# Sliding-window attention with expert routing: the fourth batch's q and k cast and turned earlier, second expert layer let in later

## The chip, the cores and the metric

The kernel runs on one core of a Trainium2 chip. The metric is the device time of one execution in microseconds (us). A core has five engines that run their own instruction queues side by side: TensorE (PE, matrix products), VectorE (DVE), ScalarE (ACT), GpSimd (POOL) and SyncE (SP, which here only issues DMAs). Each takes its instructions in the order of the program and waits on semaphores for what other engines and DMAs produce.

## What is computed

Two stages, of which the second reads the first's result:

```
# attention: q, k, v of shape (8 batches, 8 heads, 576, 64)
scores = q @ k^T / sqrt(64) + slope_h * -(i - j)     where 0 <= i - j < 128, else -1e9
attn   = softmax(scores);  x = attn @ v              -> x: (4608 tokens, 512)
# routing and experts: w1 (8, 512, 1024), w2 (8, 1024, 512)
P = exp(x @ w_gate - max); 8 times: normalise rows, normalise columns, scale by 4608/8
out = sum over e of P[:, e] * (relu(x @ w1[e]) @ w2[e])
```

## The kernel before

**Tiling.** Each batch has 576 rows: four blocks of 128, and a tail of 64. The loop runs over `steps = (b, kb, u)`: 8 batches, 5 key blocks, 2 halves of the heads. One step is a half-block, numbered `at = 2 * kb + u` from 0 to 9 within its batch; "(2, 3)" is half-block 3 of batch 2, and batches are counted from 0, so "batch 3" is the fourth. A half-block has `scores` (PE) and `exps` (ACT, L417) for the step after, `masks` (DVE, L430: the exponentials times a table that holds the window and the slopes) and `values` (PE, L455) with its division (DVE, L465 and L466). When a block is done its rows `xsb` are transposed into `xT` (by PE and a DVE copy, L497, for batches 0 to 2 and 7; by DMA, L499, for the others).

**q and k.** They come as float32 in `load_qk` (two DMAs of 1 MB on SP, L258), are cast to fp16 in four head pairs each by `cast_qk` (q on DVE, L274; k on ACT, L276; two q casts of batches 1 and 2 on POOL, L272), and must be transposed. For batches 0 to 2 PE does it (`turn_pe`, L338). From batch 3 on (`XPE = 3`) two DMA transposes on SP do it (`turn_qk`, L288), and `order_qk` (L299) then puts columns in order: four copies on POOL for k (`kN`) and four on DVE for q (`qN`, two each behind half-blocks 6 and 7). The 64-row tails are loaded by `load_tail` (L247), cast on POOL (L306) and turned by DMA (L307) in `turn_tail`.

**Filler.** PE's spare time in the attention half is filled with the first two experts' products. A unit is four blocks of tokens (two for the first two units): eight layer-1 atoms (L103, four matmuls each, relu on ACT L115 or DVE L111), then layer-2 atoms (L125, copied out by DVE L527 or L533, stored by SP L519 three outputs later from a ring of six buffers, the name `yo`). `Filler.fill(us)` hands out atoms until a planned cost (`L1_US`, `L2_US`: 0.87 and 1.74 us for a full unit) is reached. Each half-block calls it twice, first with 1.0 and then with the rest of a budget, the planned cost of all work that is ready divided by the half-blocks that are left. As long as `filler.hold` is true no layer-2 atom is handed out. For the first two units a layer-2 atom is half a block's: four matmuls, planned at 0.87 us.

**Order.** Nothing reorders the program: each engine's queue is the order of this text. Casts and turns of the next batch stand at the end of a half-block, behind its `values`, its filler work and its v load (L361); v blocks are cast on POOL (L371) one batch ahead.

Of the kernel before, what the change touches and what calls it, by code (L numbers as in the profile page):

```python
# [14 lines left out]
def kernel(  # L15
# [139 lines left out]
    XPE, YO = 3, 6  # L155
# [60 lines left out]
    if True:  # L216
# [23 lines left out]
        def spin_alone(n):  # L240
            spins[0] += 1
            spin(aps.tile([P, GT], FP32, name=f"psJ_{spins[0]}", tag="pmm", bufs=4), n)
# [21 lines left out]
        def cast_qk(b, j, which=(1, 0), pool=False):  # L264

            if b not in c16s:
                c16s[b] = per.tile([P, 2, RI, H, Dh], FP16, name=f"c16_{b}", tag="a8", bufs=8)
            for n in which:
                src = raw[b][n][:, 2 * j : 2 * j + 2, :].rearrange("p h (i d) -> p i h d", i=RI)
                to = c16s[b][:, n, :, 2 * j : 2 * j + 2, :]  # L270
                if pool:
                    nc.gpsimd.tensor_copy(out=to, in_=src)  # L272
                elif n == 0:
                    nc.vector.tensor_copy(out=to, in_=src)  # L274
                else:
                    nc.scalar.copy(out=to, in_=src)  # L276
# [52 lines left out]
        def turn_pe(b, kq, j):  # L329

            wide = j == NDT
            ps = aps.tile([P, RI, P], FP32 if wide else FP16, name=f"psT_{b}_{kq}_{j}", tag="pmm", bufs=4)
            for i in range(RI):
                if wide:
                    src = tails[b][:, 2 * i : 2 * i + 2, :]
                else:
                    src = c16s[b][:, kq, i, 2 * j : 2 * j + 2, :]
                nc.tensor.matmul(  # L338
                    out=ps[:, i, :],
                    lhsT=src.rearrange("p h d -> p (h d)"),  # L340
                    rhs=ident32 if wide else ident,
                    is_transpose=True,
                    start=(i == 0),
                    stop=(i == RI - 1),
                )
            if wide:
                nc.scalar.copy(out=QKT[b][2], in_=ps)
                return
            to = QKT[b][kq][:, j].rearrange("p (r i) -> p r i", i=RI)
            if kq == 0:  # L350
                nc.vector.tensor_copy(out=to, in_=ps.rearrange("p i r -> p r i"))
            else:
                nc.scalar.copy(out=to, in_=ps.rearrange("p i r -> p r i"))
# [36 lines left out]
        def scores(b, kb, u):  # L390

            nk, nn = sizes(kb)
            ps = aps.tile([P, 2, 2, 2 * P], FP32, name=f"psS_{b}_{kb}_{u}", tag="psS", bufs=2)
            both = kb < NKB - 2
            for y in range(2):
                j = 2 * u + y
                for hb in range(2):
                    n = 2 * P if both else nk
                    nc.tensor.matmul(  # L399
                        out=ps[0:nk, hb, y, 0:n],  # L400
                        lhsT=cols(b, 1, j, hb, kb),
                        rhs=cols(b, 0, j, hb, kb, 1 + both),
                    )
                for hb in range(2):
                    if nn and not both:
                        nc.tensor.matmul(
                            out=ps[0:nk, hb, y, nk : nk + nn],
                            lhsT=cols(b, 1, j, hb, kb),
                            rhs=cols(b, 0, j, hb, kb + 1),
                        )  # L410
            pss[b, kb, u] = ps
# [61 lines left out]
        def by_pe(b):  # L473
            return b < XPE or b == B - 1
# [192 lines left out]
        for n, (b, kb, u) in enumerate(steps):  # L667
            nxt = steps[n + 1] if n + 1 < len(steps) else None
            at = 2 * kb + u
            left = ((8 if b < XPE else 10) - at) % 10 + 1  # L670
            budget = filler.backlog() / (11 if (b, at) == (XPE, 0) else left)
            if b == 0:
                budget = 0.0
            if nxt:
                if nxt[0] < XPE and nxt[1:] == (RI - 2, 1):
                    turn_pe(nxt[0], 0, NDT)
                if nxt == (1, 0, 0):
                    filler.ready = RI
                    spin_alone(6)
                    for _ in range(NFT):  # L680
                        filler.take()
                    cast_qk(1, 0)
                    cast_qk(1, 1)
                    for j in range(NDT):
                        turn_pe(1, 1, j)
                        turn_pe(1, 0, j)
                        if j < 2:
                            cast_qk(1, j + 2, (1,))
                        filler.take()
                if nxt == (2, 0, 0):  # L690
                    filler.fill(11.0)
                    cast_qk(2, 0)
                    cast_qk(2, 1)
                    for j in range(NDT):
                        turn_pe(2, 1, j)
                        turn_pe(2, 0, j)
                        if j < 2:
                            cast_qk(2, j + 2, (1,))
                        filler.fill(1.0)
                if n == 0:  # L700
                    scores(*nxt)
                elif nxt[2] == 0:
                    scores(*nxt)
                    scores(*nxt[:2], 1)
                exps(*nxt)
            got = filler.fill(1.0) if b else 0.0
            if nxt:
                masks(*nxt)
            values(b, kb, u)
            if n > 0 and u == 0 and by_pe(steps[n - 1][0]):  # L710
                turn_x(*steps[n - 1][:2])
            if u == 1 and n // 2 + NKB < B * NKB:
                cast_v(n // 2 + NKB)
            filler.fill(budget - got)
            if at == 0 and b > XPE:
                filler.ready = 4 * b
            if at < 8 and b < XPE:
                filler.ready = 4 * b + at // 2
            if at == 8 and b < XPE:
                filler.ready = 4 * b + 4  # L720
            if u == 1 and not by_pe(b):
                turn_x(b, kb)
            if u == 1:
                if kb == 1 and b > 0:
                    gates(4 * b - 4, 4 * b)
                if n // 2 + NKB + 1 < B * NKB:
                    load_v(n // 2 + NKB + 1)
            if b == 0 and at == 5:
                load_weights(1)
            if (b, at) == (1, 8):  # L730
                filler.allowed.add(1)
            if (b, at) == (1, 5):
                for j in (2, 3):
                    cast_qk(2, j, (0,), True)
            if (b, at) == (1, 1):
                filler.hold = False
            if (b, at) == (0, 9):
                load_qk(2, 2)
            if (b, at) == (0, 7):
                homes(1)  # L740
            if (b, at) == (1, 3):
                homes(2)
            if 1 <= b < B - 2 and at == 3:
                load_qk(b + 2)
            if XPE <= b + 1 < B - 1 and at >= 8:
                cast_qk(b + 2, at - 8)
            if XPE <= b + 1 < B:
                late = 2 if b + 1 == XPE else 0
                if late and at < 2:
                    cast_qk(b + 1, at)  # L750
                if late <= at < late + 2:
                    cast_qk(b + 1, at - late + 2)
                if at == late + 1:
                    turn_qk(b + 1)
                    order_qk(b + 1, 1, range(NDT))
                if at == 5:
                    turn_tail(b + 1)
                if at in (6, 7):
                    order_qk(b + 1, 0, range(2 * at - 12, 2 * at - 10))
            if b < B - 1 and at == (1 if b > 1 else 5) and b:  # L760
                load_tail(b + 1)
            if 10 * b + at >= 66:
                i = 10 * b + at - 66
                if i % 8 == 0:
                    home_last(2 + i // 8)
                (load_w2 if i % 8 < 4 else load_w1)(2 + i // 8, i % 4, 4)
            if (b, at) == (7, 0):
                todo += sums_of(2, *extras(2))
            if b == 7 and at >= 5:
                some(1)  # L770
# [270 lines left out]
        for n in range(N):  # L1041
# [5 lines left out]
            if late:  # L1047
                finish(units[n - 2][0])
                late = []
# [16 lines left out]
            if ends(n - 1):  # L1066
                late = pairs[2] + pairs[3]
# [37 lines left out]
```

## Time and profile before

| | us |
|---|---|
| three runs | 1060.18, 1054.64, 1059.56 (median 1059.56) |
| the profiled execution | 1057.3 |
| its span, first to last instruction | 1055.4 |
| PE busy in it | 1037.4 |
| DVE, ACT, POOL busy | 633.4, 433.5, 82.3 |
| mean granted PE clock | 0.998 |

In the profile a row of a timeline is: start in us, duration in us, engine, source line, operation, output<-input, partitions x elements and type, number of instructions merged, and in brackets the engine's idle time before it with what ended that wait. A row of a window table is: the window, its length, the busy time of each engine (with instructions), the granted clock as a share of full speed, DMA share, GB/s. SPq rows are DMA issues on SP's queue: the duration is that of the issue, not of the transfer.

Batch 1 begins at about 33 us, batch 2 at 72, batch 3 at 107; attention ends near 280 us, and the rest is the remaining six experts.

### The profile page before, as it was taken

What the parts mean: (1) busy time and instruction counts of PE and PEld (TensorE: products, weight loads), DVE (VectorE), ACT (ScalarE), POOL (GpSimd) and SP (SyncE); (2) the same over time, 40 slices, a digit from 0 to 9 for tenths busy, and PEclk for the clock granted to TensorE, in tenths of its full rate; (3) what the DMA queues carried; (4) which work ended last, traced back from release to release, by engine and by line L of the source; (5) the groups of instructions that cost most, each with busy time, mean ns of one, the idle gap of its engine ahead of it and who ended that gap; (6) DMA issues with size and microseconds to landing.
All of it is one profiled execution on the core that took longest, in us unless ns stands there. A gap on an engine that the chain in (4) does not pass through costs nothing.

```text
span 1055.4 us, 21220 instructions
## 1 busy us (share of the span) xinstructions
PE 1037.4 (98%) x9042; PEld 802.5 (76%) x9042; DVE 633.4 (60%) x1170; ACT 433.5 (41%) x718; POOL 82.3 (8%) x143
## 2 busy tenths in 40 slices
PE   8899999999999999999999999999999999999998
PEld 5545444444444888888888888888888888888887
DVE  5726566655687665655655655655655555556555
ACT  7555554555332333333333333333333333333332
POOL 1212133334100000000000000000000000000000
PEclk9999999999999999999999999999999999999999
DMA  9995598969991510210210220220220220220240
GB/s 254 222 245 151 98 208 214 205 141 176 193 207 55 111 46 26 71 53 19 71 60 13 71 65 8 71 55 16 71 69 3 71 71 2 71 70 2 71 91 20
DMA packets 166174, 98.55 MB, mean 93 GB/s; under 512 B 85024, under 2 KB 157504, under 8 KB 166080
## 3 DMA queue, kind: packets, MB, share of 16 engines
q1 hardware_dynamic: 151344, 79.21, 29.1%
q0 software_dynamic: 14304, 17.84, 10.6%
q8 instruction: 70, 1.15, 0.4%
q10 hardware_dynamic: 432, 0.16, 0.1%
q14 instruction: 24, 0.20, 0.1%
HBM read 87.74 MB, written 19.02 MB: 101 GB/s over the span
## 4 chain that ended last, share of the span: by engine, by line
PE 84%; DMA 1%; DVE 0%; issue 0%; SPq 0%; DVEq 0%
PE psh L892 35%; PE psS_m L947 31%; PE psy L125 8%; PE psh L103 8%; PE psN L455 1%; DMA pbc<-ptd 1%; PE psS L399 1%; PE psy L1012 0%; PE psG L505 0%; DVE yo L533 0%; DVE aux L876 0%; PE psX L486 0%; PE psC L817 0%; DVE pt L430 0%; PE psP L832 0%
## 5 line engine op out<-in xcount | busy, mean ns | idle before, releaser
L899 ACT ACTIVATE hs<-psh 128x512 f16<-128x512 f32 x432 | 257.9, 597 | 453.6 <-PE psh L892 372.6
L892 PE MATMUL psh<-aux,w1l 128*128 128x256 f16 x2880 | 372.6, 273 | 0.5 <-DVE aux L876 0.5
L892 PEld LDWEIGHTS <-w1l 128*128 128x128 f16 x2880 | 281.5, 98 | 33.9 <-issue 0.8
L947 PEld LDWEIGHTS <-hs 128*128 128x128 f16 x2568 | 251.0, 98 | 29.3
L904 DVE TENSOR_TENSOR hs<-hs 128x1024 f16<-128x1024 f16 x107 | 74.1, 693 | 274.4 <-ACT hs L899 274.4
L947 PE MATMUL psS_m<-w2l,hs 128*128 128x256 f16 x1440 | 186.6, 273 | 0.0
L103 PE MATMUL psh<-xT,w1t 128*128 128x512 f16 (+1 forms) x608 | 141.5, 372 | 2.8 <-DVE xT L497 2.4
L125 PE MATMUL psy<-w2t,hT 128*128 128x512 f16 x576 | 134.3, 380 | 1.4 <-DMA w2t<-in_moe_w_dram 1.4
L876 DVE TENSOR_TENSOR aux<-xT,pbc 128x1024 f16<-128x1024 f16 x108 | 131.6, 1219 | 2.8 <-DMA pbc<-ptd 2.8
L115 ACT ACTIVATE hT<-psh 128x512 f16<-128x512 f32 (+1 forms) x144 | 83.5, 586 | 107.0 <-PE psh L103 106.5
L125 PEld LDWEIGHTS <-hT 128*128 128x128 f16 x576 | 53.5, 98 | 62.3 <-DMA w2t<-in_moe_w_dram 1.5
L103 PEld LDWEIGHTS <-w1t 128*128 128x128 f16 x608 | 55.2, 99 | 54.9 <-issue 8.3
L533 DVE CAST yo<-psy 128x512 f16<-128x512 f32 x68 | 46.8, 690 | 62.9 <-PE psy L125 62.6
L417 ACT ACTIVATE pt<-psS 128x1024 f16<-128x1024 f32 (+2 forms) x80 | 67.7, 852 | 39.0 <-PE psS L399 33.0
L993 DVE TENSOR_TENSOR acc<-acc,psS_m 128x256 f32<-128x256 f32 (+1 forms) x162 | 74.4, 505 | 12.3 <-PE psS_m L947 11.1
L947 PE MATMUL psS_m<-more,hs 128*128 128x256 f16 x576 | 74.7, 273 | 0.0
L892 PE MATMUL psh<-aux,w1t 128*128 128x256 f16 x576 | 74.7, 273 | 0.0
L907 DVE TENSOR_TENSOR hs<-hs 128x1024 f16<-128x1024 f16 x107 | 73.2, 684 | 0.0
L430 DVE TENSOR_TENSOR pt<-pt,mask 128x1024 f16<-128x1024 f16 (+2 forms) x80 | 53.0, 663 | 33.2 <-ACT pt L417 33.1
L892 PEld LDWEIGHTS <-w1t 128*128 128x128 f16 x576 | 56.3, 98 | 6.6
L568 POOL DMA_DIRECT2D w2t<-in_moe_w_dram x2 | 1.8, 878 | 705.6 <-PE psS_m L947 670.1
L455 PEld LDWEIGHTS <-pt 128*128 128x128 f16 (+2 forms) x576 | 28.2, 100 | 26.3 <-DVE pt L430 7.7
(89 smaller groups left out, 675.2 us busy)
## 6 DMA issues: line engine op xcount, KB each, us to landing
pbc<-ptd SPq DMA_DIRECT2D x108, 128.0 KB, 4.3
y<-ysp SPq DMA_DIRECT2D x36, 256.0 KB, 4.6
ysp<-yo SPq DMA_DIRECT2D x68, 128.0 KB, 2.9
v<-in_v_dram SPq DMA_DIRECT2D x32, 256.0 KB, 4.6
out_dram<-acc SPq DMA_DIRECT2D x31, 256.0 KB, 2.5
q<-in_q_dram SPq DMA_DIRECT2D x5, 1024.0 KB, 6.2
k<-in_k_dram SPq DMA_DIRECT2D x5, 1024.0 KB, 9.2
w2t<-in_moe_w_dram POOLq DMA_DIRECT2D x4, 1024.0 KB, 12.5
```

Of the source, the lines that this page charges most:

```text
L103: nc.tensor.matmul(out=ps[:, 0:nt], lhsT=w1ts[e][:, dt, P * ft : P * ft + P], rhs=xT[:, b0 : b0 + nb, dt, :], start=(dt == 0), stop=(dt == ...
L115: nc.scalar.activation(out=st["hT"][:, ft, 0:nt], in_=ps[:, 0:nt], func=AF.Relu)
L125: nc.tensor.matmul(out=ps, lhsT=st["hT"][:, ft, P * ms : P * ms + P], rhs=w2ts[e][:, ft, :], start=(ft == 0), stop=(ft == NFT - 1),)
L417: nc.scalar.activation(out=pt[0:nk, :, 0 : nk + nn], in_=ps[0:nk, :, :, 0 : nk + nn].rearrange("p a y n -> p (a y) n"), func=AF.Exp, scale ...
L430: nc.vector.tensor_tensor(out=pt[0:nk, :, 0:w], in0=pt[0:nk, :, 0:w], in1=mask[0:nk, hs, 0:w], op=ALU.mult)
L876: nc.vector.tensor_tensor(out=xs(n).rearrange("p (d b t) -> p d b t", d=NDT, b=2), in0=xT[:, 2 * g : 2 * g + 2].rearrange("p b d t -> p d ...
L892: nc.tensor.matmul(out=ps[:, f, :], lhsT=W1L[e][:, dt, P * ft : P * ft + P], rhs=xs(n)[:, HB * dt : HB * dt + HB], start=(dt == 0), stop=( ...
L899: nc.scalar.activation(out=h[n][:, 2 * i : 2 * i + 2, :], in_=ps, func=AF.Relu)
L904: nc.vector.tensor_tensor(out=t[:, NFT : NFT + NF2, :], in0=a[:, 0:NF2, :], in1=a[:, NF2:NFT, :], op=ALU.add)
L907: nc.vector.tensor_tensor(out=t[:, NFT + NF2 : 2 * NFT, :].rearrange("p f n -> p (f n)").rearrange("p (f t) -> p f t", t=P), in0=a[:, :, P ...
L947: nc.tensor.matmul(out=Ms[g, bank][:, half, :], lhsT=left(n, m, f), rhs=W2L[e][RIGHT[m]][:, f, :], start=(e == 2 and f == 0 and half == 0) ...
L993: nc.vector.tensor_tensor(out=a, in0=a, in1=p2, op=op)
```

## The change

Two edits in the loop over half-blocks. First, `filler.hold` is cleared at the end of half-block 2 of batch 1 instead of half-block 1. Second, the casts of batch 3 during batch 2: before, one head pair of q and k at the end of each of half-blocks 0, 1, 2 and 3, and the DMA transposes and POOL copies at the end of half-block 3. After, head pairs 0, 1 and 2 at the end of half-block 0, head pair 3 at the end of half-block 1, and there the transposes and the POOL copies. For batches 4 to 7 the calls and their places stay as they were.

```diff
-            if (b, at) == (1, 1):
+            if (b, at) == (1, 2):
                 filler.hold = False
...
             if XPE <= b + 1 < B:
-                late = 2 if b + 1 == XPE else 0
-                if late and at < 2:
-                    cast_qk(b + 1, at)
-                if late <= at < late + 2:
-                    cast_qk(b + 1, at - late + 2)
-                if at == late + 1:
+                if at == 0 and b + 1 == XPE:
+                    cast_qk(b + 1, 0)
+                    cast_qk(b + 1, 1)
+                if at < 2:
+                    cast_qk(b + 1, at + 2)
+                if at == 1:
                     turn_qk(b + 1)
                     order_qk(b + 1, 1, range(NDT))
```

## The prediction

> **What bounds the kernel now.** I read the page first, then the table of ten-microsecond windows, then the timelines of the engines around the place where half-blocks of batch 2 are cast and where batch 3 begins.
>
> ```profile
> span 1055.4 us, 21220 instructions
> PE 1037.4 (98%) x9042; PEld 802.5 (76%) x9042; DVE 633.4 (60%) x1170; ACT 433.5 (41%) x718; POOL 82.3 (8%) x143
> ```
>
> TensorE (PE) is busy for 1037.4 of 1055.4 us. All that a reordering can win is the 18 us in which PE stands, and time in which it runs at a reduced clock. The second half of the kernel does not change at all, so the place to look is the attention half, and there the windows show one that stands out:
>
> ```profile
> 10.00:20.00 10.00, 8.23 (x111) 5.10 (x109) 7.92 (x19) 8.50 (x12) 4.16 (x10) 1.00 1.25 208
> 90.00:100.00 10.00, 10.00 (x94) 5.38 (x92) 4.43 (x11) 5.95 (x10) 0.33 (x1) 1.00 0.68 138
> 100.00:110.00 10.00, 7.41 (x70) 3.83 (x68) 9.42 (x20) 2.29 (x4) 6.73 (x9) 1.00 0.21 57
> 110.00:120.00 10.00, 9.65 (x58) 4.12 (x56) 3.44 (x9) 6.11 (x10) 1.78 (x4) 0.83 0.25 65
> ```
>
> The columns are PE, weight load, DVE, ACT, POOL, then the granted clock and DMA. From 100 to 110 us PE is busy 7.41 of 10 us, the least of the eighteen windows up to 180 us, while DVE is at 9.42; just before, DVE is at 4.43. From 110 to 120 the mean clock is 0.83, which over 10 us is 1.7 us of PE time lost. No other window there shows a clock under 1.00. This is the end of batch 2 and the start of batch 3, in PE's own order:
>
> ```profile
> 104.88 0.31 PE L455 MATMUL psN<-v,pt 128*64 128x65 f16 x4
> 106.25 0.31 PE L455 MATMUL psN<-v,pt 64*64 64x65 f16 x4 [1.07 <-DVE pt L430]
> 107.03 1.07 PE L399 MATMUL psS<-qN,kN 64*128 64x256 f16 x8
> 109.47 1.02 PE L103 MATMUL psh<-xT,w1t 128*128 128x512 f16 x4 [1.38 <-DVE xT L497]
> 110.91 4.45 PE L103 MATMUL psh<-xT,w1t 128*128 128x512 f16 x12
> 115.20 0.29 PE L455 MATMUL psN<-v,pt 128*128 128x65 f16 x4
> 150.39 2.59 PE psh L103 x12
> ```
>
> PE waits 1.07 us for a mask product and 1.38 us for the copy of the last transposed block into xT. Then twelve 512-wide matmuls stretch from 110.91 to 115.20, 4.29 us, where twelve like them take 2.59 elsewhere: 1.70 us too long, the loss which the clock column shows. So 2.45 us of waits and 1.70 us of clock, 4.15 us together, lie at this joint.
>
> Why DVE is late is in its own rows:
>
> ```profile
> 96.69 0.56 DVE L430 TENSOR_TENSOR pt<-pt,mask 128x768 f16<-128x768 f16 x1 [1.32 <-ACT pt L417]
> ...
> 100.47 0.69 DVE L533 CAST yo<-psy 128x512 f16<-128x512 f32 x1 [1.03 <-PE psy L125]
> 101.08 1.07 DVE L430 TENSOR_TENSOR pt<-pt,mask 128x768 f16<-128x768 f16 x1
> ...
> 102.95 2.03 DVE L299 COPY qN<-qk 128x512 f16<-128x512 f16 x2
> ...
> 105.50 0.70 DVE L430 TENSOR_TENSOR pt<-pt,mask 64x256 f16<-64x256 f16 x1
> ...
> 106.67 1.09 DVE L299 COPY qN<-qk 128x512 f16<-128x512 f16 x2
> ...
> 108.27 0.27 DVE L430 TENSOR_TENSOR pt<-pt,mask 64x256 f16<-64x256 f16 x1
> ...
> 109.01 0.41 DVE L497 COPY xT<-psX 128x512 f16<-128x512 f16 x1
> ```
>
> The same mask product of 128x768 takes 0.56 us at 96.69 and 1.07 at 101.08. The pair of qN copies takes 1.09 us at 106.67 and 2.03 at 102.95. The 64x256 mask takes 0.27 us at 108.27 and 0.70 at 105.50. The long ones all lie where POOL works on batch 3's kN copies or on what stood behind them:
>
> ```profile
> 99.67 4.85 POOL L299 COPY kN<-qk 128x512 f16<-128x512 f16 x4 [9.95 <-DMA qk<-c]
> ```
>
> Excess on DVE: 0.51 + 0.94 + 0.43 = 1.88 us, in one unbroken queue from 100.47 to the xT copy at 109.01.
>
> **The change, part 1: when batch 3 is turned.** The text of the change speaks of pairs; the code puts three casts of each of q and k (head pairs 0, 1, 2) behind half-block 0 and the fourth behind half-block 1, with both DMA transposes and the four POOL copies. No instruction is added or removed.
>
> ```profile
> 81.21 0.42 DVE L274 CAST c<-q 128x512 f16<-128x512 f32 x1
> 82.98 0.69 DVE L533 CAST yo<-psy 128x512 f16<-128x512 f32 x1 [1.35 <-PE psy L125]
> ...
> 84.74 0.42 DVE L274 CAST c<-q 128x512 f16<-128x512 f32 x1
> ...
> 92.08 0.42 DVE L274 CAST c<-q 128x512 f16<-128x512 f32 x1
> ```
>
> On DVE the cast at 81.21 is followed by 1.35 us of idle; two more casts of 0.42 fit, 0.84 us, so the next one (82.98) is not late. The last q cast then is the one at 84.74, ending at 85.16, where before it was that at 92.08, ending at 92.50. That is 7.34 us earlier.
>
> ```profile
> 79.43 0.63 ACT L276 CAST c<-k 128x512 f16<-128x512 f32 x1
> 80.93 1.02 ACT L417 ACTIVATE pt<-psS 128x1024 f16<-128x1024 f32 x1 [0.87 <-PE psS L399]
> ...
> 107.46 1.02 ACT L417 ACTIVATE pt<-psS 128x1024 f16<-128x1024 f32 x1 [3.35 <-PE psS L399]
> ```
>
> On ACT two more casts of at most 0.63 stand behind the one at 79.43 and end by 81.3; the exponential that started at 80.93 after 0.87 us of idle moves by up to 0.4 us. The mask that uses it waited on DVE behind the output copy at 82.98 anyway, so I cost this at nothing; without that cover it would be 0.4 us.
>
> ```profile
> 73.13 1.24 SPq L247 DMA_DIRECT2D t<-in_q_dram  x1
> ...
> 75.14 6.51 SPq L519 DMA_DIRECT2D ysp<-yo  x2
> ...
> 82.87 0.84 SPq L258 DMA_DIRECT2D k<-in_k_dram  x1
> 92.52 4.65 SPq L288 DMA_TRANSPOSE qk<-c  x2
> ```
>
> SP is an in-order queue. The transposes waited for the last cast and started at 92.52; now they start at 85.2 and hold SP for 4.65 us, to 89.9. They have moved ahead of the tail loads (73.13), the y stores (75.14), a v load and batch 4's q and k loads (82.87), so all of these now issue after 89.9. The k load needs
>
> ```profile
> k<-in_k_dram SPq DMA_DIRECT2D x1, 1024.0 KB, 9.2
> ```
>
> 9.2 us to land. Issued at about 93 it is there at 102.2; its first reader is an ACT cast ahead of the exponential at 107.46, which moves to about 105.6. That leaves 3 us, so I cost it at nothing. The stores are priced among the rivals.
>
> POOL gets the copies 7.34 us earlier: 92.3 to 97.2 instead of 99.67 to 104.52. The v casts queued behind them feed batch 3, which begins about 107 us, and the one ahead-of-time cast that now waits behind them has as long. DVE, at 4.43 of 10 us in that window, has room for a slowdown of the size seen, 1.88 us, without PE noticing.
>
> Without the excess, DVE's queue from 100.47 reaches the 64x256 mask at about 104.1 and PE, at 104.88, goes straight on: the wait of 1.07 is gone. The xT copy, ending at 109.42, ends at 107.54. PE gets there at about 106.3, since the scores at 107.03 need the second pair of qN copies, which end at 107.76 - 1.88 = 105.9. So a wait of 1.2 us stays, and the matmul of 109.47 starts at 107.6. **Gain 1.9 us**; bounds 0 (what POOL casts then slows DVE as much) and 2.45 (both waits vanish).
>
> [...]
>
> **Part 2: the clock.** PE's matmul at 109.47 starts after a stretch of 4.6 us with 2.45 us of waits. With 1.25 us less idle, the window from 100 to 110 would have PE busy some 8.66 of 10 us; the window from 10 to 20 has 8.23 and a clock of 1.00. I take the drop to vanish: **1.70 us**; bounds 0 and 1.70.
>
> **Part 3: layer 2 one half-block later.** At half-block 2 of batch 1 the filler gives one layer-2 atom (four matmuls):
>
> ```profile
> 37.10 0.29 PE L455 MATMUL psN<-v,pt 128*128 128x65 f16 x4
> 38.78 1.04 PE L125 MATMUL psy<-w2t,hT 128*128 128x512 f16 x4 [1.38 <-DMA w2t<-in_moe_w_dram]
> ```
>
> It waits 1.38 us for w2. Now the filler gives nothing there, since layer 1 has run out. Eight atoms of 0.87 are owed by the planner's own costs, 6.96, and the budget is what is owed over the half-blocks left: in half-block 3 that is 6.96/6 = 1.16 us, one atom; in half-block 4 it is 6.09/5 = 1.22, of which 0.35 is left after the first atom, enough by its rule for a second one. From half-block 5 on the order is the old one. So one atom moves by two half-blocks. PE then waits at the old place for other things:
>
> ```profile
> 37.65 0.68 DVE L430 TENSOR_TENSOR pt<-pt,mask 128x1024 f16<-128x1024 f16 x1
> ...
> 38.45 0.42 DVE L466 TENSOR_TENSOR xsb<-psN,rden 128x256 f16<-128x256 f32 x1
> ```
>
> The mask ends at 38.33, so PE waits from 37.40 to 38.4, 0.95 to 1.0 us instead of 1.38, and again 0.25 us or so for xsb, ready at 38.87. The moved 0.87 us are spent later, in front of no wait that would hide them. **Gain 0.3 us**, near 1.38 - 1.0; bounds -0.9 (the atom uncovered at its new place and nothing won) and 1.38.
>
> Sum: 1.9 + 1.7 + 0.3 = 3.9 us. The profiled execution took 1057.3 us (1055.4 of span and 1.9 around it), so 1053.4. The three runs have a median of 1059.56; the four times known (1060.18, 1054.64, 1059.56, 1057.3) have a mean of 1057.9. Taking the 3.9 off that I forecast **1054.0 us**.
>
> **Rivals.** *The clock drops all the same.* For it: a wait of 1.2 us stays at the same place. Against it: windows with as little PE work kept a clock of 1.00. It would leave 2.2 us, thus 1055.7. [...]
>
> *The contention moves along.* POOL's v casts, kept back by the early copies, fall on the same DVE stretch, or masks in the quiet window become the wait. Against it: DVE's 4.43 of 10. Then only part 3 remains: 1057.6.
>
> *Slower: the stores behind the transposes.* Outputs rotate through six buffers; the output copied on DVE at 100.47 needs the buffer whose store is the first at 75.14. A store lands
>
> ```profile
> ysp<-yo SPq DMA_DIRECT2D x68, 128.0 KB, 2.9
> ```
>
> 2.9 us after issue. Behind transposes (to 89.9) and two tail loads (at most 1.24 each) it lands by about 96, 4.5 us ahead of need. It decides from 4.5 us more on SP. That SP can be held is shown by a single load in batch 1:
>
> ```profile
> 49.15 10.07 SPq L258 DMA_DIRECT2D q<-in_q_dram  x1
> ```
>
> If each transpose took 10.07 us, SP would be 15.5 us later, the copy at 100.47 would wait 11 us, and masks queue behind it: 1057.3 + 11 - 0.3 = 1068. Against it: they took 4.65 for both.
>
> *It does not do what it says:* the casts still end with half-block 3's. The queue order excludes this unless ACT or DVE were full there; they are not.
>
> **How the numbers follow.** Forecast 0.56; clock drops 0.22; contention moves 0.13; stores 0.06; the rest 0.03. One half percent, 5.3 us, is about what a measurement of this kernel can tell from no change; the runs before differ by 5.5 us. Against the median 1059.56 the forecast is 5.6 us faster, against the mean 3.9, so a little under half of the forecast's chance (0.25) is faster by over 0.5%, and of the clock's rival a quarter (0.06): 0.31. Slower by over 0.5%: the stores and a little of the contention case, 0.08. Within: 0.61. The range runs from 1050.5 (the lowest run, 1054.64, less 3.9 and rounded) to 1059.0 (the contention case, 1057.6, and 1.4 for the spread of runs); it takes in the bounds of the parts.
>
> **What would show it.** Transposes on SP starting near 85 and kN copies on POOL near 92; in the window 100 to 110 no 1.07 us mask and no 2.03 us qN pair; PE's first layer-1 matmul of batch 3's start near 107.3; a clock of 1.00 from 110 to 120; no PE wait on w2, and four matmuls more behind half-block 4 of batch 1. Wrong would be: copies early but the xT copy as late as ever; a clock under 1.00 at another place; SP issuing the stores after 96.

## The result and the profile after

| | median, us | runs | lowest to highest |
|---|---|---|---|
| before | 1059.37 | 18 | 1054.64 to 1061.93 |
| after | 1054.63 | 18 | 1052.86 to 1058.07 |

The ratio, of the means (1054.72 to 1059.02), is 0.9959, with a 95% interval of 0.9948 to 0.9971: 4.3 us, 0.41% faster, where 1054.0 and 3.9 us were forecast. The ratio itself lies within the 0.5% that was called the bound; its interval reaches just beyond it. One execution of before among the 35 that stand beside e1 to e4 below was slow throughout (1795.9 us, mean clock 0.556) and is left out of every comparison.

The profiled execution of after took 1058.07 us, the slowest of the 18, so its span is no shorter than that of before. From the page of after:

```profile
span 1055.2 us, 21217 instructions
PE 1037.0 (98%) x9042; PEld 803.7 (76%) x9042; DVE 632.4 (60%) x1170; ACT 433.9 (41%) x718; POOL 81.0 (8%) x143
```

Ten-microsecond windows of after (columns as in the table of before):

```profile
40.00:50.00 10.00, 9.10 (x104) 5.33 (x103) 5.81 (x15) 4.10 (x5) 5.19 (x12) 0.83 0.93 210
90.00:100.00 10.00, 10.00 (x106) 5.63 (x106) 5.26 (x13) 6.28 (x10) 3.94 (x4) 1.00 1.03 199
100.00:110.00 10.00, 9.37 (x82) 4.89 (x79) 8.64 (x21) 3.32 (x6) 3.42 (x8) 1.00 1.02 274
110.00:120.00 10.00, 8.87 (x60) 4.13 (x60) 4.48 (x13) 6.70 (x12) 1.65 (x4) 1.00 0.22 59
```

The window from 110 to 120 has a clock of 1.00 instead of 0.83. The window from 100 to 110 has PE busy for 9.37 us instead of 7.41, but this trace runs late, so that part of the joint has moved out of that window. In a second profile of the same kernel (f1_whole below), which runs less late, it is 8.71, near the 8.66 of the forecast:

```profile
100.00:110.00 10.00, 8.71 (x80) 4.58 (x78) 8.56 (x21) 2.46 (x5) 2.05 (x5) 1.00 1.07 267
```

But in the first profile the clock is 0.83 from 40 to 50, in batch 1, and a clock under 1.00 at another place is one of the signs that the prediction named for being wrong. The timelines of POOL and PE of after show what happened there:

```profile
40.18 0.61 POOL L371 CAST v<-v 128x512 f16<-128x512 f32 x1 [8.32 <-DMA v<-in_v_dram]
40.90 0.55 PE L455 MATMUL psN<-v,pt 128*128 128x65 f16 x7 [2.90 <-POOL v L372]
```

POOL sat idle for 8.32 us until the DMA of a v block landed, and PE waited 2.90 us for the cast. Batch 2 and all behind it therefore stand some 3 us later in this trace than they would otherwise (batch 1 takes 39.73 us here and 36.48 in f1, as read below); this lies well ahead of the joint of batches 2 and 3. At the joint itself, PE's timeline reads:

```profile
107.94 0.56 PE L455 MATMUL psN<-v,pt 128*64 128x65 f16 x8
...
108.75 0.61 PE L399 MATMUL psS<-qN,kN 64*128 64x256 f16 x8
110.70 1.02 PE L103 MATMUL psh<-xT,w1t 128*128 128x512 f16 x4 [1.34 <-DVE xT L497]
...
112.14 2.76 PE L103 MATMUL psh<-xT,w1t 128*128 128x512 f16 x12
114.75 0.29 PE L455 MATMUL psN<-v,pt 128*128 128x65 f16 x4
```

The row of 107.94 stands for those of 104.88 and 106.25 before, with no wait between: the wait of 1.07 is gone. The wait for xT is 1.34 (before 1.38). The twelve 512-wide matmuls take 2.61 us from 112.14 to 114.75 (before 4.29). The stretch from the first of these rows to the last I call the joint: 10.32 us before (104.88 to 115.20), 6.81 after (107.94 to 114.75). So the joint is 3.51 us shorter.

DVE's and POOL's timelines of after, with the rows that answer to the slow ones:

```profile
99.75 1.32 DVE L430 TENSOR_TENSOR pt<-pt,mask 128x768 f16<-128x768 f16 x1 [1.17 <-ACT pt L417]
...
104.14 0.55 DVE L430 TENSOR_TENSOR pt<-pt,mask 128x768 f16<-128x768 f16 x1
...
105.49 1.10 DVE L299 COPY qN<-qk 128x512 f16<-128x512 f16 x2
...
107.11 0.27 DVE L430 TENSOR_TENSOR pt<-pt,mask 64x256 f16<-64x256 f16 x1
...
107.85 1.10 DVE L299 COPY qN<-qk 128x512 f16<-128x512 f16 x2
...
109.46 0.31 DVE L430 TENSOR_TENSOR pt<-pt,mask 64x256 f16<-64x256 f16 x1
...
110.24 0.41 DVE L497 COPY xT<-psX 128x512 f16<-128x512 f16 x1
96.06 4.59 POOL L299 COPY kN<-qk 128x512 f16<-128x512 f16 x4 [17.04 <-DMA qk<-c]
```

Both qN pairs take 1.10 us (one took 2.03), the mask of 128x768 at 104.14 takes 0.55 (1.07), and the mask of 64x256 at 107.11 takes 0.27 (0.70). The mask beside the copies now is the one at 99.75, and it takes 1.32. DVE had been idle for 1.17 us before it, and PE does not wait for it.

### The profile page after: what moved, and what is told of

The parts are those of the page before. It is cut to its first block, busy times and chain, and to the rows that moved or that the text cites. A ratio compares the mean times of both kernels' runs of the same rounds, so it can differ in the third digit from the quotient of the medians.

```text
span 1055.2 us, 21217 instructions
## 1 busy us (share of the span) xinstructions
PE 1037.0 (98%) x9042; PEld 803.7 (76%) x9042; DVE 632.4 (60%) x1170; ACT 433.9 (41%) x718; POOL 81.0 (8%) x143
## 4 chain that ended last, share of the span: by engine, by line
PE 85%; DVE 0%; issue 0%
PE psh L892 36%; PE psS_m L947 31%; PE psy L125 8%; PE psh L103 8%; PE psN L455 1%; PE psS L399 1%; PE psy L1012 0%; PE psG L505 0%; DVE yo L533 0%; PE psX L486 0%; PE psC L817 0%; DVE pt L430 0%; PE psP L832 0%; DVE L_sb L820 0%; PE psS L406 0%; DVE acc L1020 0%
```

## The experiments

The length of the joint, read from PE's timeline of each kernel, sums up their profiles. "Clock loss" is one minus the listed mean clock, times the span, averaged over the runs of that kernel (34 of before, 18 of after, 12 each of e1 to e4, 6 of e6); the clock is listed to three places, so that the mean of many runs is good to some tenths; it covers the whole execution, the end of the kernel too. The third column gives the joint up to its first 512-wide matmul, which leaves the clock out: in none of these profiles does PE work at a reduced clock in the joint ahead of that matmul.

| kernel | joint, us | up to the first 512-wide matmul | wait for mask + for xT | clock, 110 to 120 | clock loss per run, us |
|---|---|---|---|---|---|
| before | 10.32 | 4.59 | 1.07 + 1.38 | 0.83 | 3.11 |
| e1_hold_only | 9.93 | 4.45 | 0.92 + 1.38 | 0.83 | 2.82 |
| e3_copies_twice | 11.40 | 4.46 | 0.92 + 1.38 | 0.69 | 3.70 |
| e4_spin | 8.56 | 4.52 | 0.98 + 0.39 | 1.00 | 0.97 |
| e2_turn_only | 6.76 | 2.72 | 0 + 1.30 | 1.00 | 0.53 |
| after (its second profile, f1_whole below) | 6.75 | 2.71 | 0 + 1.29 | 1.00 | 0.76 |
| e6_q_at_5 (its second profile, f2_q5 below) | 6.10 | 2.05 | 0 + 0.63 | 1.00 | 0.70 |

The rows of f1_whole from which its line is read:

```profile
106.10 0.56 PE L455 MATMUL psN<-v,pt 128*64 128x65 f16 x8
...
108.81 1.02 PE L103 MATMUL psh<-xT,w1t 128*128 128x512 f16 x4 [1.29 <-DVE xT L497]
...
112.85 0.29 PE L455 MATMUL psN<-v,pt 128*128 128x65 f16 x4
```

### The two edits apart

**e1_hold_only**: before, with the first edit alone.

```diff
-            if (b, at) == (1, 1):
+            if (b, at) == (1, 2):
                 filler.hold = False
```

> The kernel before with only the second layer let in one half-block later; batch 3 is cast and turned as before. Theory (the turn carries the gain): between -0.3 and +0.5 us against before, ratio 0.9995 to 1.0005, because PE at half-block 2 of batch 1 then waits for a mask, xsb or a v block instead of w2; the 1.07 us mask, the 2.03 us qN pair and both waits at the joint of batches 2 and 3 stay, and the clock falls there. Rival (the wait on w2 and what follows from it is the larger part in unprofiled runs): -2 us or more, ratio 0.998 or less.

Measured: ratio 0.9992 (0.9978 to 1.0005), median 1058.59 against 1058.40. The joint has all its old features: waits of 0.92 and 1.38, and a clock of 0.83. The edit alone has no gain that these runs can tell.

**e2_turn_only**: after, with the first edit undone.

```diff
-            if (b, at) == (1, 2):
+            if (b, at) == (1, 1):
                 filler.hold = False
```

> The kernel before with only the casts and turns of batch 3 moved to half-blocks 0 and 1 of batch 2; layer 2 comes in as before. Theory: 3.6 us faster than before (1.9 of waits, 1.7 of clock), ratio about 0.9966, and equal to or a little better than the whole change; at the joint one wait of 1.2 to 1.4 us on the xT copy is left and the clock is 1.00. Rival (the w2 wait matters): only 1 to 2 us faster, ratio 0.998 to 0.999, and clearly slower than the whole change.

Measured: ratio 0.9965 (0.9953 to 0.9978), median 1055.16. The earlier turn carries the gain: the joint of 6.76 is as short as with both edits.

### Is it the copies beside DVE?

**e3_copies_twice**: e2_turn_only, with the four kN copies made a second time at the end of half-block 5. They write the same values again, at the time at which the kernel before made them.

```diff
                 if at == 5:
                     turn_tail(b + 1)
+                    if b + 1 == XPE:
+                        order_qk(b + 1, 1, range(NDT))
```

> The turn moved alone, and in addition the four POOL copies of batch 3's k done a second time (same values) behind half-block 5 of batch 2, so that POOL copies at the place where it did in the kernel before, while casts and DMA transposes stay early. Theory (POOL's copies slow DVE there, and that is the price): the long masks and the 2 us qN pair come back, PE waits about 2.4 us at the joint again and the clock falls: within 0.7 us of the kernel before, so 3 us slower than the turn alone. Rival (the gain comes from the earlier casts or transposes themselves, or from SP): as fast as the turn alone, ratio 0.9966.

Measured: ratio 0.9994 (0.9981 to 1.0007). No gain is left that these runs can tell. The timelines of POOL, DVE and PE in its profile:

```profile
100.33 4.85 POOL L299 COPY kN<-qk 128x512 f16<-128x512 f16 x4
101.75 1.07 DVE L430 TENSOR_TENSOR pt<-pt,mask 128x768 f16<-128x768 f16 x1
...
103.61 2.03 DVE L299 COPY qN<-qk 128x512 f16<-128x512 f16 x2
112.52 4.58 PE L103 MATMUL psh<-xT,w1t 128*128 128x512 f16 x12
```

and two of its windows:

```profile
100.00:110.00 10.00, 7.55 (x70) 3.83 (x68) 8.86 (x20) 2.29 (x4) 5.85 (x7) 0.97 0.97 247
110.00:120.00 10.00, 9.70 (x46) 3.92 (x47) 3.76 (x10) 4.42 (x8) 1.25 (x4) 0.69 0.00 0
```

The mask takes 1.07 and the qN pair 2.03 again, to the hundredth what they took before. POOL copies that nobody needs bring the loss back, while the casts and the transposes stay early: the joint up to the first 512-wide matmul is 4.46 us again, against 2.72 without them. So what the change gains is that POOL no longer copies beside DVE; a gain of the earlier casts and transposes by themselves is not seen.

### Is the clock a part of its own?

**e4_spin**: before, with eight matmuls on a block of ones put in ahead of the first filler call of half-block 9 of batch 2. Nothing reads their result, and nothing else is moved.

```diff
+            if (b, at) == (2, 9):
+                spin_alone(8)
```

> The kernel before with nothing moved, and eight 256-wide dummy matmuls (0.9 us) put into PE's queue at the joint of batches 2 and 3, ahead of the matmul that waits 1.38 us for the xT copy. Theory (the reduced clock follows from too little PE work in that stretch): the wait shrinks to about 0.5 us with the dummies in it, the clock stays at 1.00 from 110 to 120, and the time falls by up to 1.7 us, ratio about 0.9985. Rival (the clock falls by chance of its phase, whatever PE does): the clock still falls in the same share of runs, and the time is that of before.

Measured: ratio 0.9975 (0.9961 to 0.9990), median 1055.09. PE's timeline:

```profile
108.82 1.05 PE L236 MATMUL psJ<-ones 128*128 128x256 f16 x8
110.27 1.02 PE L103 MATMUL psh<-xT,w1t 128*128 128x512 f16 x4 [0.39 <-DVE xT L497]
...
111.71 2.76 PE L103 MATMUL psh<-xT,w1t 128*128 128x512 f16 x12
114.31 0.29 PE L455 MATMUL psN<-v,pt 128*128 128x65 f16 x4
```

and the window:

```profile
110.00:120.00 10.00, 9.31 (x62) 4.34 (x62) 4.90 (x13) 6.93 (x12) 1.60 (x4) 1.00 0.27 70
```

The slow DVE rows are all still there (a qN pair takes 2.03 us, a 64x256 mask 0.70), and xT is as late as before. PE fills 1 us of that wait with work of no use. The twelve matmuls then take 2.60 us, and the loss of clock falls from 3.11 to 0.97 us per run. So the clock is a cost of its own, and it comes from PE's idleness at this place. 1 - 0.9975 is 2.6 us, with an interval of 1.1 to 4.1: more than the 1.7 us expected, but 1.7 lies within the interval.

### What is late next: the wait for xT

**e5_q_at_4** and **e6_q_at_5**: after, with batch 3's qN copies taken from behind half-blocks 6 and 7 to behind 4 and 5, or 5 and 6.

```diff
-                if at in (6, 7):
-                    order_qk(b + 1, 0, range(2 * at - 12, 2 * at - 10))
+                lo = 5 if b + 1 == XPE else 6
+                if at in (lo, lo + 1):
+                    order_qk(b + 1, 0, range(2 * (at - lo), 2 * (at - lo) + 2))
```

(e6; e5 has a 4 in place of the 5.)

> The whole change, and batch 3's qN copies on DVE behind half-blocks 4 and 5 of batch 2 instead of 6 and 7. Theory (what is left at the joint is DVE's queue ahead of the last xT copy, and 2.2 us of it are these copies): the wait of 1.3 us on xT goes to 0.3 or less; but both pairs now lie beside POOL's copies (92 to 99) and take 2 us each, so about 0.5 to 1.0 us is left of the gain, 1.0 us faster than the whole change at best. Rival (PE has no slack for DVE before 105 either): a mask wait of 0.5 to 1 us appears between 98 and 104 and the time is that of the whole change or 1 us above it.

> The whole change, and the qN copies behind half-blocks 5 and 6 of batch 2. Theory: only one pair leaves DVE's queue between the second last and the last xT copy, 1.0 us, so the wait of 1.3 us shrinks to 0.3, and the time is 1.0 us under that of the whole change (about 0.9950 of the kernel before), with the first pair a little slowed by POOL's casts. Rival: the wait is set by PE's own chain (xsb, transpose, copy), then it stays over 1 us and nothing is gained.

Measured: e5 0.9954 (0.9937 to 0.9971), e6 0.9949 (0.9930 to 0.9968), medians 1054.16 and 1054.26 against 1058.76 for before. The wait for xT falls to 0.75 (e5) and 0.88 (e6), where 0.3 was expected in both. In e5 the first pair of qN copies, from 97.95, lands beside the kN copies on POOL (busy for 5.48 of the 10 us from 90 to 100) and takes 2.03 us; in e6 both pairs are quick (1.13 and 1.10). What had not been foreseen is the last mask ahead of xT, first in e5 and then in e6:

```profile
107.65 0.54 DVE L430 TENSOR_TENSOR pt<-pt,mask 64x256 f16<-64x256 f16 x1
108.67 0.67 DVE L430 TENSOR_TENSOR pt<-pt,mask 64x256 f16<-64x256 f16 x1
```

It takes 0.28 us in e2, where POOL's v cast (from 106.59, 0.66 us) ends ahead of it at 107.29. The 0.54 and 0.67 here are near the 0.70 of the mask beside POOL's casts in before (105.50), so that a v cast beside it in e5 and e6 as well is my estimate. The difference in time to the whole change is too small for these runs.

### The late v block in batch 1

**e7_spin_b1**: after, with eight such matmuls ahead of the first filler call of half-block 2 of batch 1, to hold the clock there. **e8_q5_spin**: the same with e6's edit.

```diff
+            if (b, at) == (1, 2):
+                spin_alone(8)
```

> The whole change, and eight 256-wide dummy matmuls (0.9 us) in PE's queue at half-block 2 of batch 1, where the layer-2 atom was. Theory (the clock that the whole change still loses, 0.76 us a run, is lost after the thin stretch there): it falls to 0.3 us or less, the time by up to 0.5 us, since the dummies lie in a wait of 1 us or more. Rival (the moved atom is not what thins that stretch, the late v block or other places are): same time and same clock as the whole change, or 0.2 to 0.4 us slower where the dummies are not covered.

> The whole change with both: qN copies behind half-blocks 5 and 6, and the dummies in batch 1. If the two theories hold, their gains add: 1.5 us under the whole change, about 0.9945 of the kernel before. If only the copies count, 1.0 us under; if neither, the time of the whole change.

Measured: e7 0.9955 (0.9940 to 0.9970), e8 0.9942 (0.9921 to 0.9962). The loss of clock is 0.70 us per run in both, as without the matmuls. In e7's profile PE has done them and then waits all the same:

```profile
37.90 1.03 PE L236 MATMUL psJ<-ones 128*128 128x256 f16 x8
...
40.86 0.37 PE L455 MATMUL psN<-v,pt 128*128 128x65 f16 x7 [1.89 <-POOL v L372]
```

Its window from 40 to 50 has a clock of 0.83 as in after. The matmuls stand in the wait, but they are too short for it: they end at 38.93, v comes 1.89 us later, and the clock falls behind that. The expected 0.3 us or less of clock loss did not come.

### Which version is best

The whole change, e6's kernel, e8's kernel, and e6's kernel with the first edit undone, on one chip, six runs each.

> The whole change as it is, beside the other three on one chip: 0.9959 of the kernel before, as in its first comparison (0.9948 to 0.9971).

> The whole change with the qN copies behind half-blocks 5 and 6. If the 0.4 to 0.8 us that left the wait on xT are real, 0.5 us under the whole change on the same chip, 0.9954; if the first pair beside POOL takes it back, no difference.

> The same with the dummies in batch 1. The lowest so far: if that was more than chance, again 1.0 us or more under the whole change, 0.995 or less; otherwise as the one without dummies, since their clock loss was the same.

> The qN copies behind half-blocks 5 and 6 and the turn moved, but layer 2 let in as in the kernel before. If the later layer 2 is worth 0.3 us as forecast, 0.3 us over the one with it; if it costs the clock in batch 1, below it.

| kernel | median, us | ratio to before | interval |
|---|---|---|---|
| f1_whole | 1054.34 | 0.9959 | 0.9945 to 0.9974 |
| f2_q5 | 1052.79 | 0.9947 | 0.9931 to 0.9963 |
| f3_q5_spin | 1053.68 | 0.9951 | 0.9935 to 0.9966 |
| f4_q5_no_hold | 1053.62 | 0.9951 | 0.9936 to 0.9965 |

The qN copies one half-block earlier give the lowest median in this set, 1.5 us below the whole change; the intervals overlap, so that it is better than the whole change is likely and not shown. The matmuls of batch 1 add nothing that these runs can tell, and the first edit is again within the noise. The clock loss per run is 0.88, 0.70, 0.70 and 0.35 us in the order of the table: least without the first edit. With the early turn and no first edit it is 0.53 in e2 as well, and with both edits 0.70 to 0.88 in every set of runs. That the first edit costs some clock in batch 1 fits this; with 18 runs without it this is not shown. f2's timelines of DVE and PE tell what bounds the joint then:

```profile
105.20 0.69 DVE L533 CAST yo<-psy 128x512 f16<-128x512 f32 x1 [0.26 <-DMA ysp<-yo]
107.00 1.02 PE L103 MATMUL psh<-xT,w1t 128*128 128x512 f16 x4 [0.63 <-DVE xT L497]
```

The wait for xT is down to 0.63 (0.49 in e8 and 0.88 in e6, with these copies early by one half-block too). In front of it DVE now waits 0.26 us for a store out of the yo ring, which was the forecast's slower rival: it appears, small, once what stood before it is gone.

## Why the prediction was right, and where its sizes were off

**The queue (part 1).** The transposes, the store, the k load and the k cast that waits for it:

```profile
88.28 5.12 SPq L288 DMA_TRANSPOSE qk<-c  x2
...
95.25 1.08 SPq L519 DMA_DIRECT2D ysp<-yo  x2
...
98.02 0.60 SPq L258 DMA_DIRECT2D k<-in_k_dram  x1
107.72 0.62 ACT L276 CAST c<-k 128x512 f16<-128x512 f32 x1 [1.06 <-DMA k<-in_k_dram]
```

They start at 88.28, where 85.2 was forecast; in this trace batch 2 itself stands some 3 us later (POOL's copies start at 96.06 here, at 93.75 in e2 and at 92.91 in f2, where 92.3 was forecast). The next y stores issue at 95.25, even so before the 96 that was set as the limit. The casts end with half-block 1's, as read from the queue order. One cover was thinner than claimed: the k load of batch 4 was said to have 3 us to spare, and ACT's cast waited 1.06 us for it: the load issues at 98.02 here, where 93 was forecast. It cost nothing here, because ACT waits another 0.84 us behind that cast for PE's next scores.

**The contention (part 1).** 1.9 us were forecast. Measured as the joint less its clock, it is 10.32 - 1.70 = 8.62 before and 6.75 in the second profile of after, so 1.87; up to the first 512-wide matmul it is 4.59 - 2.71 = 1.88. Of this 2.45 - 1.29 = 1.16 are the two waits; the rest are short waits inside merged rows, such as the scores behind qN (1.07 us at 107.03 before, 0.61 at 108.75 after). The wait left over, forecast at 1.2, is 1.29 to 1.34. e3 shows that it is POOL's copies beside DVE: 4.46 us up to the first 512-wide matmul with them, 2.72 in e2 without. The rival "contention moves along" did happen on the masks beside the copies (1.32 at 99.75 in after, 1.35 at 97.36 in e3, against 0.56 at 96.69 before), and DVE's idle time took it, as argued against that rival.

**The clock (part 2).** The direction was right, and the rival "the clock drops all the same" did not come true at this place in any profile with the early turn, but for e3's with its second copies: with a wait of 1.29 to 1.34 left the clock is 1.00 in after, e2 and f1. But 1.70 us was a mis-sized term. The one-microsecond windows of before show what the 0.83 is made of:

```profile
111.00:112.00 1.00, 1.00 (x3) 0.33 (x4) 0.95 (x3) 0.19 (x1) 0.67 (x1) 0.52 0.60 139
112.00:113.00 1.00, 1.00 (x4) 0.36 (x3) 0.40 (x1) 0.24 (x1) 0.45 (x2) 0.50 0.90 245
113.00:114.00 1.00, 1.00 (x4) 0.40 (x3) 0.00 (x0) 0.35 (x1) 0.58 (x2) 0.50 0.03 10
114.00:115.00 1.00, 1.00 (x5) 0.36 (x4) 0.00 (x0) 0.54 (x2) 0.08 (x2) 0.78 0.00 0
```

The clock is at one half from 111.0 to 114.4, some 3.4 us, and half of that is the 1.70. In e3 the clock lost (1.00 - 0.97) x 10 + (1.00 - 0.69) x 10 = 3.4 us at the same place, twice as much, with nearly the same waits (0.92 and 1.38): it is at one half from 109.4 to 116.2, though PE is busy without a gap from 110.0 on. Most runs of before have a mean clock of 0.997 or less (22 of 34, a loss of some 3 us or more), and the profiled one has 0.998: it was one of the luckier ones, with a single such stretch. e1's profiled run had one at another place too, behind a late v block in batch 0, first in PE's timeline and then in the window:

```profile
23.30 0.54 PE L455 MATMUL psN<-v,pt 128*128 128x65 f16 x7 [1.92 <-POOL v L372]
```

```profile
20.00:30.00 10.00, 8.08 (x98) 6.42 (x94) 5.52 (x17) 4.44 (x9) 3.56 (x7) 0.83 1.19 288
```

Per run, the loss fell from 3.11 to 0.76 us, by 2.35, where 1.70 was taken, and 1.70 had been given as its upper bound. That bound was wrong: it was the loss of one execution, and the typical loss stands in the clocks of the other runs. The longest single wait at the joint is 1.38 us in before, e1 and e3 alike, and the stretch at one half is 3.4 us long in before and 6.8 in e3: the runs do not show what sets its length.

**Layer 2 later (part 3).** 0.3 us were forecast. Batch 1 of f1_whole and of e2_turn_only, PE's timelines, between the same two groups of transposes of casts, first f1:

```profile
30.43 0.70 PE L338 MATMUL psT<-ident,c 128*128 128x128 f16 x8 [0.55 <-ACT c L276]
...
40.08 0.39 PE L455 MATMUL psN<-v,pt 128*128 128x65 f16 x7 [0.96 <-DVE pt L430]
...
66.91 0.62 PE L338 MATMUL psT<-ident,c 128*128 128x128 f16 x8 [1.26 <-ACT c L276]
```

and e2:

```profile
29.81 0.70 PE L338 MATMUL psT<-ident,c 128*128 128x128 f16 x8 [0.54 <-ACT c L276]
...
66.58 0.62 PE L338 MATMUL psT<-ident,c 128*128 128x128 f16 x8 [1.25 <-ACT c L276]
```

From start to start it is 36.48 us in f1 and 36.77 in e2, so 0.29 us, and the wait in f1 is the 0.96 for the mask that was forecast (0.95 to 1.0). The layer-2 atoms are at their forecast places. But this pair alone proves little. The same stretch takes 36.58 to 37.60 us in the five profiles without the edit (before, e2, e3, e4, f4; mean 37.08). In the six with it and without added matmuls in batch 1 it takes 36.47 to 36.97 in four (f1, f2, e1, e5), and 39.33 and 39.73 in two (e6, after); their mean is 37.58. So the step is there where v comes in time, and over these profiles no gain is left of it. The times of e1 (0.8 us faster, between 2.3 faster and 0.5 slower), and of after against e2, neither show nor exclude it. What was not foreseen: with the atom gone, PE comes to `values` of the next half-block sooner, and when its v block is late it waits there. In the profiles with the edit that wait was 2.90 (after, whose same stretch is from 29.02 to 68.75), 2.63 (e6), 1.89 (e7) and 1.75 (f3; e7 and f3 behind their added matmuls), and absent in others; of the kernels without it four wait there for w2 instead (0.85 in e3 to 1.91 in f4, 1.38 before) and e2 for the mask (0.97). That the edit trades one late DMA for another is what these rows suggest; no run was made to show it.

**The sum.** 1.87 for the waits and 2.35 for the clock make 4.2, with nothing for layer 2. The means of the 18 and 18 runs differ by 1059.02 - 1054.72 = 4.3. So close a match is in part chance, since the waits come from two profiles, and the clock of before comes from the runs beside e1 to e4. That the forecast sum of 3.9 came so near is in part luck as well: the clock was taken 0.65 too small, and the 0.3 of layer 2 is not shown. Taking the gain off the mean of the four times known, not the median, brought the forecast to 1054.0; off the median it would have been 1055.7, which is 1.0 too high where 1054.0 is 0.6 too low.

## What to carry to other kernels

Where DVE is the late engine, look at what POOL does at the same time: here fp16 copies on POOL about doubled the fp16 work of DVE beside them (a mask of 128x768 from 0.56 to 1.07 us, a qN pair from 1.09 to 2.03), and moving them into a stretch in which DVE idles was worth 1.9 us without one instruction less. The thin PE work at this joint was paid for twice in the profile of before, 2.45 us as waits and 1.70 as clock behind them, and the second payment varied from run to run (mean clocks of 0.995 to 1.000 in 34 runs of before): take it from the clocks of many executions, not from one trace. Ask of a filled wait what PE reaches sooner once the filling is moved: here it was a v block that was not always there. When a wait is gone, look at once for the next one at the same place; here it was the qN copies behind which xT stood, and then the ring of stores.

## What the runs showed of the hardware that was not expected

In before the clock fell to 0.50 for 3.4 us after waits of 1.07 and 1.38 us within 5 us; with eight matmuls of no use, 1.05 us, in the second wait it stayed at 1.00 in e4's profile. Of single waits up to 1.54 us (after, at 148.27) none did it; 1.89 (e7), 1.92 (e1), 2.63 (e6) and 2.90 us (after) did, and 1.75 (f3), 1.91 (f4) and 2.37 us (e8, at 23.80) did not. So the length of the wait alone does not decide.

The seven falls that these profiles show in the attention half (one each in before, e3, after, e6 and e7, two in e1) have in common that PE was busy for 1.07 (after, 36.93 to 40.34) to 1.90 us (before, 107.60 to 111.00) of the 3.4 us ahead of the fall, a stretch as long as that at one half in before. In the joints of after, e2 and f1 the thinnest such stretch holds 2.06 to 2.11 us. But stretches as thin were also passed at 1.00 (1.03 us in e8, 20.40 to 23.80; 1.81 in after, 146.80 to 150.20), so that what else decides stays open.

Beside POOL's copies DVE's fp16 masks and copies, which lie in SBUF, took longer (masks of 128x768 1.07 us in before and 1.32 in after instead of 0.55, qN pairs 2.03 instead of 1.10), and beside its casts to fp16 too (the mask of 64x256 at 105.50 in before 0.70 instead of 0.27). The division of 128x256, which reads PSUM, did not: in before it took 0.42 us at 102.28 beside a copy, at 106.33 beside a cast and at 94.61 beside neither.
